# A softmax by blocks of token rows, a weight product in halves, and a new order of a planned stage

## The chip, the core and the metric

The kernel runs on one core of one Trainium2 chip. The metric is the device time of one execution in microseconds (us), the median over several runs. One further execution is recorded by the hardware profiler; its own time stands beside them below.

## The reference

```python
def _attn_ref(q, k, v, phi):            # 4 batches, 8 heads, 576 tokens, 64 columns, 32 memory slots
    a = softmax of phi over the tokens
    k_m, v_m = a^T k, a^T v              # pooled keys and values, 32 x 64 per head
    attn = softmax(scale * q k_m^T)      # over the 32 slots, for every token
    return attn v_m
x = attention, heads side by side       # 2304 tokens x 512
x = ((x w_a) * (x w_b)) w_out            # glu, inner width 1536
h = x w_in
return max(0.01 h, h) w_out2             # leaky, inner width 2048
```

All inputs are float32, and the kernel's planned stage and what follows split most operands into a high and a low part, so that three products (high by high, high by low, low by high) stand for one.

## The kernel before

The attention's last product and the glu's first are joined: with `vblk`, the pooled values, the kernel forms W = v_m w for each batch and each block f of 128 glu columns (`plan_w`, the product `wp`, L1183), and then one product of W with the attention weights AT gives (x w_a) and (x w_b) at once (`plan_ab`, the product `ab`, L1246, 24 of them per batch and block: two halves x of the width, two halves n of the tokens, two halves g of the heads, three passes). `copy` (ScalarE, L1263) and `mult` (VectorE, L1268) form the glu from it, and `x1p` (L1312) multiplies with w_out. W and AT are each made in two parts: ScalarE copies the high part (L1208, L1123), VectorE subtracts it for the low part (L1212, L1127).

The attention of one batch is `plan_att`. For batch 0 it pools keys and values (`km`, L771, first over k, then over v), scales them on ScalarE or VectorE (`kc`, L844, L846), turns them (`kvT`, L858) and writes `kk` and `vblk` (L882). Queries are turned in pieces (`qT`, L1014; `qL`, L970, for the last rows), the scores are `sc` (L1050, L1056), one group for each pair i of heads over all nine rows j of 64 tokens. VectorE takes the maximum (L993) and subtracts it (L1002), ScalarE forms the exponential (L1079) for two pairs at a time, VectorE sums (L1088), inverts and divides (L1100). Nine transposes `aT` (L1110), three to a bank, then bring the weights into AT. Each of these nine waits for the division of both halves of the heads.

The weights come as float32 in two halves of a word, and are joined after the load: ScalarE makes the high word (L438), GpSimd or ScalarE the low one (L446, L442), VectorE joins them (L456).

None of these instructions stands where the code names it. Each is a `Step` with an engine, a cost, what it waits for, and what it holds (a bank of `att`, `ab` or `wp`). `Plan.order` plays the steps through with these costs, and each engine gets its instructions in the order of the starts that come out. `LATE`, `FETCHED` and `LATEST` say how long after its issue a load is taken to land. `SEEDS` is a list of shuffles of the due times, applied one after the other. Where TensorE has nothing ready before 27 us, `run` puts in a product of ones (`warm`, L1680, 512 or 256 wide). Behind the planned stage, from L1690 on, the second layer is written out by hand.

```python
    LATE, FETCHED, LATEST = (4.0, 2.3), 1.2, 5.2
    WARM = 27.0
            s_at = add(PE, 0.325, att_t, s_soft, take=hold, uses=[s_users], kind="t")
```

## Time and profile before

| what | us |
|---|---|
| median of 3 runs | 738.47 |
| lowest, highest | 737.46, 738.53 |
| profiled execution, its own time | 738.45 |
| its span | 736.4 |
| TensorE busy (`warm` among it) | 729.4 |
| VectorE, ScalarE, GpSimd busy | 579.1, 413.7, 20.1 |

The span is the time between the first and the last instruction of the profile; the profiled execution's own time holds 2.05 us more, around it. A row of a timeline gives start, length, engine, line, operation, the tile written and the tiles read, and how many instructions are merged. A product of float32 operands shows twice in it, so that `x16` on `wp` is eight products. Neighbouring products overlap, and the distance from one start to the next is what one takes of the engine. A product with ones is a busy TensorE in all views.

### The profile page before, as it was taken

How to read it: one execution, taken by the hardware profiler on the slowest of the kernel's cores; microseconds unless marked ns; L12 is line 12 of the kernel's file. 1: busy time of each engine (PE TensorE's matmuls, PEld its weight loads, DVE VectorE, ACT ScalarE, POOL GpSimd, SP SyncE). 2: the span in 40 equal slices, each digit the busy share in tenths (PEclk: the TensorE clock that was granted, in tenths of full speed). 3: DMA queues.
4: the chain of work that ended last, by engine and by line, in shares of the span. 5: the costliest groups of instructions: out<-in, count | busy, mean ns of one | idle time of the engine just before them, and what ended most of it. 6: DMA issues, size and time to landing. Idle time of an engine off the chain costs nothing.

```text
span 736.4 us, 14535 instructions
## 1 busy us (share of the span) xinstructions
PE 729.4 (99%) x5391; PEld 654.2 (89%) x5391; DVE 579.1 (79%) x1196; ACT 413.7 (56%) x915; POOL 20.1 (3%) x38
## 2 busy tenths in 40 slices
PE   8999999999999999999999999999999999999997
PEld 5787887988889798888899999999999999999987
DVE  5987786967809999998746767998866997877797
ACT  3886684866729787856414455644444743454442
POOL 1210000001300000000000000000000000000000
PEclk9999999999999999999999999999999999999999
DMA  9995267474605989876527877778987777997493
GB/s 312 359 395 184 77 219 246 158 241 131 218 3 199 319 311 320 296 239 250 206 93 253 263 252 250 254 256 256 295 286 258 261 245 249 288 289 246 152 304 88
DMA packets 87495, 175.27 MB, mean 238 GB/s; under 512 B 7553, under 2 KB 36737, under 8 KB 87425
## 3 DMA queue, kind: packets, MB, share of 16 engines
q1 hardware_dynamic: 86736, 173.77, 70.6%
q8 instruction: 42, 0.69, 0.4%
q10 hardware_dynamic: 688, 0.59, 0.3%
q14 instruction: 29, 0.23, 0.1%
HBM read 140.25 MB, written 34.08 MB: 237 GB/s over the span
## 4 chain that ended last, share of the span: by engine, by line
PE 93%; DVE 3%; DMA 2%; ACT 1%; issue 0%; SPq 0%; DVEq 0%
PE h L1750 24%; PE x1p L1312 19%; PE ab L1246 19%; PE o L1850 15%; PE o L1854 8%; PE wp L1183 3%; DMA stage<-in_moe_w_b_dram 1%; PE sc L1050 1%; PE qT L1014 1%; PE km L758 1%; PE km L771 1%; PE aT L1110 1%; PE warm L1680 1%; DMA phi_t<-in_phi_dram 1%; DVE w2o L1434 0%; PE h L1825 0%
## 5 line engine op out<-in xcount | busy, mean ns | idle before, releaser
L1850 PE MATMUL o<-w2o,S 128*128 128x512 f32 (+1 forms) x504 | 177.1, 386 | 0.0
L1246 PEld LDWEIGHTS ab<-AT,W 128*128 128x128 f32 x1152 | 154.8, 188 | 7.0 <-ACT W L1208 2.5
L1246 PE MATMUL ab<-AT,W 128*128 128x288 f32 x1152 | 160.0, 297 | 0.2
L1312 PE MATMUL x1p<-G,wo 128*128 128x512 f32 (+1 forms) x720 | 156.5, 372 | 0.0
L1802 ACT ACTIVATE S<-g 128x384 fp32r<-128x384 f32 x168 | 87.6, 523 | 99.2 <-PE o L1850 85.9
L1312 PEld LDWEIGHTS x1p<-G,wo 128*128 128x128 f32 x720 | 123.5, 189 | 22.2 <-issue 0.8
L1750 PE MATMUL h<-T,ring 128*128 128x384 f32 x720 | 141.8, 335 | 0.0
L1854 PE MATMUL o<-w2o,S 128*128 128x256 f32 x492 | 137.6, 280 | 0.0
L1750 PEld LDWEIGHTS h<-T,ring 128*128 128x128 f32 x720 | 120.9, 188 | 4.1
L1803 DVE TENSOR_TENSOR S<-g,S 128x384 fp32r<-128x384 f32 x168 | 91.5, 553 | 40.4 <-ACT S L1802 40.2
L1850 PEld LDWEIGHTS o<-w2o,S 128*128 128x128 f32 x504 | 93.7, 188 | 14.5
L1854 PEld LDWEIGHTS o<-w2o,S 128*128 128x128 f32 x492 | 92.8, 189 | 0.0
L1872 DVE TENSOR_TENSOR C<-C,o 128x768 f32<-128x768 f32 x75 | 71.0, 949 | 13.9 <-ACT C L1876 7.9
L1750 PE MATMUL h<-B,ring 128*128 128x384 f32 x288 | 57.2, 336 | 0.0
L1793 DVE TENSOR_TENSOR g<-g 128x384 f32<-128x384 f32 x96 | 52.3, 552 | 2.9 <-ACT g L1760 2.4
L1750 PEld LDWEIGHTS h<-B,ring 128*128 128x128 f32 x288 | 48.8, 188 | 1.6
L438 ACT ACTIVATE stage<-stage 128x512 f32<-128x512 f32 x68 | 46.0, 686 | 5.6 <-DMA stage<-in_moe_w_in_dram 2.5
L1268 DVE TENSOR_TENSOR g<-a_sb,ab 128x288 f32<-128x288 f32 x96 | 42.1, 446 | 5.8 <-PE ab L1246 4.8
L1263 ACT COPY a_sb<-ab 128x288 f32<-128x288 f32 x96 | 38.3, 402 | 12.9 <-PE ab L1246 12.5
L1283 ACT ACTIVATE G<-g 128x576 fp32r<-128x576 f32 x48 | 33.2, 691 | 12.6 <-DVE g L1268 12.5
L1212 DVE TENSOR_TENSOR W<-wp,W 128x256 fp32r<-128x256 f32 (+1 forms) x75 | 35.1, 491 | 5.5 <-ACT W L1208 4.7
L1208 ACT ACTIVATE W<-wp 128x256 fp32r<-128x256 f32 (+1 forms) x75 | 30.3, 449 | 15.9 <-PE wp L1183 8.4
(143 smaller groups left out, 737.5 us busy)
## 6 DMA issues: line engine op xcount, KB each, us to landing
w2o<-a_scr SPq DMA_DIRECT2D x168, 256.0 KB, 3.8
ring<-a_scr SPq DMA_DIRECT2D x72, 512.0 KB, 4.4
stage<-in_moe_w_out_dram SPq DMA_DIRECT2D x28, 512.0 KB, 5.2
a_scr<-w2o SPq DMA_DIRECT2D x24, 512.0 KB, 3.7
a_scr<-a_out SPq DMA_DIRECT2D x24, 512.0 KB, 4.1
stage<-in_moe_w_in_dram SPq DMA_DIRECT2D x16, 512.0 KB, 5.2
stage<-in_moe_w_a_dram SPq DMA_DIRECT2D x12, 512.0 KB, 8.4
stage<-in_moe_w_b_dram SPq DMA_DIRECT2D x12, 512.0 KB, 7.5
```

The costliest lines, as they stand in the source:

```text
L438: act.activation(out=x, in_=x, func=ACTF.Prelu, scale=2.0 ** -112, alpha=2.0 ** 32)
L1246: pe.matmul(out=c[x, n][:, :HS], lhsT=W[b, f][:, hw, g, 128 * x:128 * x + 128], rhs=AT[b][:, g, ha, n * HS:(n + 1) * HS], start=(g == 0 an ...
L1263: act.copy(c["sb"][:, n], c[0, n][:, :HS])
L1268: dve.tensor_tensor(out=c["g"][:, n], in0=c["sb"][:, n], in1=c[1, n][:, :HS], op=ALU.mult)
L1312: pe.matmul(out=c["ps"], lhsT=wo_t[f][:, hw, 128 * m:128 * m + 128], rhs=G[f][:, hg, first:first + n], start=(f == fs[0] and (hw, hg) == P ...
L1750: pe.matmul(out=out, lhsT=ring[i % 2, part][:, o, kp, hw], rhs=x[:, hx], start=fresh and kp == 0 and (hw, hx) == PASSES[0], stop=kp == 1 a ...
L1793: dve.tensor_tensor(out=t, in0=x, in1=y, op=op)
L1802: act.activation(out=t[:, 0], in_=src, func=ACTF.Copy)
L1803: dve.tensor_tensor(out=t[:, 1], in0=src, in1=t[:, 0].bitcast(F32), op=ALU.subtract)
L1850: pe.matmul(out=dst[:, u, :y - x], lhsT=hi, rhs=wide[:, x:y], start=fresh and x == 0, stop=False, skip_group_check=True,)
L1854: pe.matmul(out=dst[:, u, :256], lhsT=lo, rhs=t[:, 0], start=False, stop=q == 3, skip_group_check=True,)
L1872: o_adds.append(lambda x=x: dve.tensor_tensor(out=total[name], in0=total[name], in1=x, op=ALU.add))
```

## The change

For batch 0 alone, `block(k)` does the softmax by rows of tokens and not by pairs of heads: rows 0 to 4 for all eight heads, then rows 5 to 8. Each block has two score groups (four pairs of heads, two pairs in a bank), its own sum, inverse and division. `qL` turns row 4 in place of row 8. The transposes `aT` go in groups of three, two and four rows, the first two waiting for the first block alone.

For the first block of the glu (b, f) = (0, 0), W is made in two halves, one for w_a and one for w_b, each with a tile of its own (`plan_w_first`), and its 24 products are no longer planned by three passes for each g, but by four steps: high by high for one g, the same for the other, low W by high AT for both, high W by low AT for both, and each waits for its own part.

`FETCHED` goes from 1.2 to 0.4 and `LATEST` from 5.2 to 4.8, and the list of shuffles is another, of 95 in place of 53. So the order changes throughout the planned stage. The code of the other batches is moved under an `else`.

```diff
-    LATE, FETCHED, LATEST = (4.0, 2.3), 1.2, 5.2
-    SEEDS = (683652, 560159, 530175, 125177, 433488, 159828, 165231, 686446, 405802, 158260, 349165, 253408, 67255,
...
-             250324)
+    LATE, FETCHED, LATEST = (4.0, 2.3), 0.4, 4.8
+    SEEDS = (522689, 898407, 926596, 464601, 390815, 382426, 130910, 244497, 699877, 414418, 82018, 903452, 136320,
...
+             532242, 848879, 434245, 992645)
...
-            def ql_t(i=i, n=n, hold=hold):
+            def ql_t(i=i, n=n, hold=hold, last=NR - 1 if b else 4):
...
-                        out=ps[:, 128 * x:128 * x + 128], in_=c["q"][:, i + x, (NR - 2) * D:NR * D], identity=ident
+                        out=ps[:, 128 * x:128 * x + 128], in_=c["q"][:, i + x, (last - 1) * D:(last + 1) * D],
+                        identity=ident,
...
-        for i in range(NQ):
-            hold = Hold(banks, 1)
-            qt_before, qt_users = qt0 if b == 0 else qt2 if i > 1 else plan.slot("qT", 2)
...
+        def block(k):
+            r0, nr = (0, 5) if k == 0 else (5, 4)
+            qt_before, qt_users = qt0
+            size = 2 * nr * M
+            s_ex = []
+            for h in range(2):
+                hold = Hold(banks, 1)
+
+                def q_t(h=h, hold=hold):
+                    ps = c["qTp", k, h] = bank(hold, "qT")
+                    for x in range(4):
+                        first = 128 * (2 * k + x % 2) + 64 * k
+                        pe.transpose(
+                            out=ps[:, 128 * x:128 * x + 128], in_=c["q"][:, 2 * h + x // 2, first:first + 128],
+                            identity=ident,
+                        )
+
...
+                    copy(
+                        c["qT"][:, 2 * h:2 * h + 2, 2 * k:2 * k + 2].rearrange("p i j x -> p i (j x)"),
+                        c["qTp", k, h].rearrange("p (i x) -> p i x", i=2),
+                    )
...
+                s = add(PE, 0.43, q_t, [ld_q[h]] + qt_before, take=hold, uses=[q_users], kind="t", n=8)
+                s_q = copied(q_copy, 512, [s] + qt_before, give=[hold], uses=[qt_users])
+                hold = Hold("att" if h else banks, 1)
...
+                def score(h=h, hold=hold):
+                    ps = bank(hold, "sc")[:, :size].rearrange("p (i x) -> p i x", i=2)
+                    for x in range(4):
+                        i, jj = 2 * h + x // 2, x % 2
+                        for g in range(NG):
+                            rows = slice(64 * g, 64 * g + 64)
+                            pe.matmul(
+                                out=ps[rows, x // 2, 64 * jj:64 * jj + 64], lhsT=c["qT"][:, i, 2 * k + jj, rows],
+                                rhs=kk[g][:, i].rearrange("p n m -> p (n m)"), start=True, stop=True,
+                            )
...
+                s_sc = add(
+                    PE, 0.22 if k else 0.33, score, s_kk + [s_q] + ([] if k else [s_ql[2 * h]]) + s_before, take=hold,
+                    uses=kk_users + [qt_users] + ([] if k else [ql_users]), n=16 if k else 24, kind="s"
+                )
...
+                    dve.tensor_reduce(out=c["m", k, h], in_=c["o", k, h], axis=AX.X, op=ALU.max)
+
+                s_max = add(DVE, t_dve(size), row_max, [s_sc] + m_before, uses=[m_users])
...
+                    return c["s"][:, r0:r0 + nr, 2 * h:2 * h + 2]
+
...
+                def less_row(h=h, part=part):
+                    bc = c["m", k, h].unsqueeze(3).to_broadcast([128, nr, 2, M])
+                    dve.tensor_tensor(out=part(), in0=c["o", k, h], in1=bc, op=ALU.subtract)
+
+                s_les = add(DVE, t_dve(size), less_row, [s_max] + s_before, give=[hold], uses=[s_users, m_users])
+                s_ex.append(add(
+                    ACT, t_act(size),
+                    lambda part=part: act.activation(out=part(), in_=part(), func=ACTF.Exp, scale=scale),
+                    [s_les], uses=[s_users],
+                ))
...
+                dve.tensor_reduce(out=c["m2", k], in_=c["s"][:, r0:r0 + nr], axis=AX.X, op=ALU.add)
+
+            s_rs = add(DVE, t_dve(2 * size), row_sum, s_ex + m_before, uses=[s_users, m_users])
+            s_eps = add(
...
+            def divide():
+                bc = c["m2", k].unsqueeze(3).to_broadcast([128, nr, NQ, M])
+                dve.tensor_tensor(
+                    out=c["s"][:, r0:r0 + nr], in0=c["s"][:, r0:r0 + nr], in1=bc, op=ALU.mult
+                )
+
+            return add(DVE, t_dve(2 * size), divide, [s_rec], port=True, uses=[s_users, m_users])
...
+        s_soft = []
+        if b == 0:
+            s_soft = [block(0), block(1)]
+            s_soft.insert(0, s_soft[0])
+        else:
+            for i in range(NQ):
...
-        for i in range(2):
-            part = slice(2 * i, 2 * i + 2)
-            s_ex = add(
-                ACT, t_act(576),
-                lambda part=part: act.activation(
-                    out=c["s"][:, :, part], in_=c["s"][:, :, part], func=ACTF.Exp, scale=scale
-                ),
-                s_att[part], uses=[s_users],
-            )
...
-        for i in range(3):
+        for i, (r0, nr) in enumerate(((0, 3), (3, 3), (6, 3)) if b else ((0, 3), (3, 2), (5, 4))):
...
-                for jj in range(3):
+                for jj in range(nr):
...
-            s_at = add(PE, 0.325, att_t, s_soft, take=hold, uses=[s_users], kind="t")
-            s_hi = add(ACT, t_act(384), high, [s_at], give=[hold])
-            ends += [s_hi, add(DVE, t_dve(384), low, [s_hi], give=[hold], early=8.0 if b else 0.0)]
+            s_at = add(PE, 0.108 * nr, att_t, s_soft if b else s_soft[i:i + 1], take=hold, uses=[s_users], kind="t")
+            s_hi = add(ACT, t_act(128 * nr), high, [s_at], give=[hold])
+            ends += [s_hi, add(DVE, t_dve(128 * nr), low, [s_hi], give=[hold], early=8.0 if b else 0.0)]
+        if b == 0:
+            att_ends.extend(ends)
...
-        for fs in ((0,), (1,)) if apart else ((0, 1),):
+        for fs, x in (((0,), 0), ((0,), 1), ((1,), None)) if apart else (((0, 1), None),):
             c = {}
-            where = "att" if apart and fs == (0,) else spot
+            where = "att" if apart and x != 1 else spot
             wide = where == "wp"
             holds = [Hold(where, 2 * len(fs)) for g in range(1 if wide else NG)]
...
+            made = [y for i in fs for n in range(2) if n == x or x is None for y in conv_end["wab", f + i, n]]
             s.append(main(
-                0.853 if len(fs) > 1 else 0.48, product, (ready if fs[-1] else ready[:NG]) + made + done_att + s, take=holds,
+                0.853 if len(fs) > 1 else 0.48 if x is None else 0.26, product, ready + made + done_att + s, take=holds,
...
-                def place(i=i):
+                def place(i=i, x=x):
+                    if x is not None and (b, f + i, x) not in W:
+                        W[b, f + i, x] = keep.tile([128, 2, NG, 128], F32R, tag=f"G{2 + x}", name="W")
+                    if x is not None:
+                        return W[b, f + i, x]
...
+    def plan_w_first(x):
+        s, high, low, holds, wide = w_before[0, 0, x]
+        before, users = plan.slot(f"G{2 + x}")
+        hi, lo = [], []
+        for k, hold in enumerate(holds):
+            n = 256 if wide else 128
+            hi.append(plan.add(ACT, 0.1 + t_act(n), lambda k=k: high(k), [s] + before, give=[hold], uses=[users]))
+            lo.append(plan.add(DVE, t_dve(n), lambda k=k: low(k), [hi[-1]], give=[hold], uses=[users]))
+        w_first[x] = hi, lo, users
 
     def plan_w_parts(b, f):
+        if (b, f) == (0, 0):
+            plan_w_first(0)
+            plan_w_first(1)
+            return
...
-            ends = [hi, lo] if k == 0 or (b, f) == (0, 0) else ends + [hi, lo]
-            for g in (k,) if (b, f) == (0, 0) else range(NG):
+            ends = [hi, lo] if k == 0 else ends + [hi, lo]
+            for g in range(NG):
                 w_end[b, f, g] = ends
...
-                    steps.append(main(
-                        0.3975, product, w_end[b, f, g] + att_end[b, g, n] + steps,
-                        take=None if g else out, uses=[w_used[b, f]],
-                    ))
+                    if (b, f) != (0, 0):
+                        steps.append(main(
+                            0.3975, product, w_end[b, f, g] + att_end[b, g, n] + steps,
+                            take=None if g else out, uses=[w_used[b, f]],
+                        ))
+                if (b, f) == (0, 0):
+
+                    def passes(todo, x=x, n=n, out=out):
+                        for g, hw, ha in todo:
+                            if todo[0] == (0, 0, 0):
+                                c[x, n] = bank(out, "ab")
+                            pe.matmul(
+                                out=c[x, n][:, :HS], lhsT=W[b, f, x][:, hw, g], rhs=AT[b][:, g, ha, n * HS:(n + 1) * HS],
+                                start=(g, hw, ha) == (0, 0, 0), stop=(g, hw, ha) == (1, 0, 1),
+                            )
+
+                    hi, lo, users = w_first[x]
+                    for todo, need in (
+                        ([(0, 0, 0)], hi[:1] + att_ends[2 * n:2 * n + 4:2]), ([(1, 0, 0)], hi),
+                        ([(0, 1, 0), (1, 1, 0)], lo), ([(0, 0, 1), (1, 0, 1)], att_ends[2 * n + 1:2 * n + 5:2]),
+                    ):
+                        steps.append(main(
+                            0.1325 * len(todo), lambda todo=todo, passes=passes: passes(todo), need + steps,
+                            take=None if steps else out, uses=[users], n=2 * len(todo),
+                        ))
```

On TensorE, around the first glu product, the order before is this, from the last score group on (`km` here pools v, `wp` is the product for f = 0 and then for f = 1):

```order
L1680 MATMUL warm<-const-float32-1.0 128x512
L1680 MATMUL warm<-const-float32-1.0 128x256
L771 MATMUL km<-kv_t,e 64x128 x36
L1680 MATMUL warm<-const-float32-1.0 128x256
L858 MATMUL kvT<-ident,kc 128x2x32 x2
L1680 MATMUL warm<-const-float32-1.0 128x256
L1183 MATMUL wp<-wab,vblk 32x256 x8
L1110 MATMUL aT<-ident,s 128x128 x9
L1680 MATMUL warm<-const-float32-1.0 128x256
L1183 MATMUL wp<-wab,vblk 32x256 x8
L1246 MATMUL ab<-AT,W 128x288 x36
L1183 MATMUL wp<-wab,vblk 32x512 x8
```

And after the change, the second `wp` of 16 instructions being the two halves for f = 0:

```order
L1831 MATMUL warm<-const-float32-1.0 128x512
L774 MATMUL km<-kv_t,e 64x128 x36
L1219 MATMUL aT<-ident,s 128x128 x3
L861 MATMUL kvT<-ident,kc 128x2x32 x2
L1219 MATMUL aT<-ident,s 128x128 x2
L1294 MATMUL wp<-wab,vblk 32x128 x16
L1219 MATMUL aT<-ident,s 128x128 x4
L1395 MATMUL ab<-AT,W 128x288 x12
L1294 MATMUL wp<-wab,vblk 32x256 x8
L1395 MATMUL ab<-AT,W 128x288 x10
L1376 MATMUL ab<-AT,W 128x288 x9
```

The first five transposes moved ahead of `wp`, into the places of two fillers, the last four stand right before the first `ab`, and the `wp` of f = 1 moved behind twelve of the products.

On VectorE, at the same place, before, from the last difference of a score on (`m` is the maximum and then the sum's inverse, `wab` a joined weight block):

```order
L1088 TENSOR_REDUCE m_323<-s 128x18
L1100 TENSOR_TENSOR s<-s,m_290 128x9x64
L1092 TENSOR_SCALAR m_323<-m_323 128x18
L1095 RECIPROCAL m_323<-m_323 128x18
L1100 TENSOR_TENSOR s<-s,m_323 128x9x64
L456 SCALAR_TENSOR_TENSOR wab<-stage 128x4x128
L1212 TENSOR_TENSOR W<-wp,W 128x256
L456 SCALAR_TENSOR_TENSOR wab<-stage 128x4x128
L1127 TENSOR_TENSOR AT<-aT,AT 128x3x2x64 x2
L1212 TENSOR_TENSOR W<-wp,W 128x256
L1127 TENSOR_TENSOR AT<-aT,AT 128x3x2x64
```

And after:

```order
L1106 TENSOR_TENSOR s<-s,m_288 128x640
L1094 TENSOR_REDUCE m_338<-s 128x16
L1098 TENSOR_SCALAR m_338<-m_338 128x16
L1101 RECIPROCAL m_338<-m_338 128x16
L459 SCALAR_TENSOR_TENSOR wab<-stage 128x4x128
L1106 TENSOR_TENSOR s<-s,m_338 128x512
L1236 TENSOR_TENSOR AT<-aT,AT 128x3x2x64
L1236 TENSOR_TENSOR AT<-aT,AT 128x2x2x64
L1327 TENSOR_TENSOR W<-wp,W 128x128 x2
L1327 TENSOR_TENSOR W<-wp,W 128x256
L459 SCALAR_TENSOR_TENSOR wab<-stage 128x4x128 x2
L1236 TENSOR_TENSOR AT<-aT,AT 128x4x2x64
```

The division is 640 and then 512 columns wide. A join of a weight block now stands between the second inverse and the second division, and the first differences of AT have moved ahead of those of W.

On ScalarE, from the last exponential on, before:

```order
L1079 ACTIVATE s<-s 128x9x64 x2
L844 ACTIVATE kc<-km,r 128x2x64 x2
L438 ACTIVATE stage<-stage 128x512
L882 COPY vblk<-kvT 128x128
L438 ACTIVATE stage<-stage 128x512
L1208 ACTIVATE W<-wp 128x256 x2
L1123 ACTIVATE AT<-aT 128x3x2x64 x2
L442 ACTIVATE stage<-stage 128x512
L1123 ACTIVATE AT<-aT 128x3x2x64
```

And after:

```order
L1085 ACTIVATE s<-s 128x4x64 x2
L847 ACTIVATE kc<-km,r 128x2x64 x2
L441 ACTIVATE stage<-stage 128x512
L1232 ACTIVATE AT<-aT 128x3x2x64
L885 COPY vblk<-kvT 128x128
L441 ACTIVATE stage<-stage 128x512
L1232 ACTIVATE AT<-aT 128x2x2x64
L1323 ACTIVATE W<-wp 128x128 x2
L1323 ACTIVATE W<-wp 128x256
L441 ACTIVATE stage<-stage 128x512
L1232 ACTIVATE AT<-aT 128x4x2x64
```

The high part of AT's first three rows moved ahead of the copy of `vblk`, and that of the next two ahead of W.

## Rows read from the trace of the kernel before

**Rows 1.** Head and part 1 of the page: busy time, share, instructions

```profile
span 736.4 us, 14535 instructions
...
PE 729.4 (99%) x5391; PEld 654.2 (89%) x5391; DVE 579.1 (79%) x1196; ACT 413.7 (56%) x915; POOL 20.1 (3%) x38
```

**Rows 2.** Waits of TensorE: who waited for whom; total, times, longest us

```profile
PE mxT L637 <- DVE mx L613: 1.0, 1, 1.0
...
PE kvT L858 <- ACT kc L844: 0.5, 1, 0.5
...
PE aT L1110 <- DVE s L1100: 0.2, 1, 0.2
```

**Rows 3.** Busy us by engine in two stretches, granted clock, DMA share, GB/s

```profile
27.09:382.05 354.96, 354.39 (x3030) 307.69 (x3023) 277.06 (x624) 238.34 (x556) 14.58 (x19) 1.00 0.64 223
...
4.00:6.00 2.00, 1.09 (x3) 0.19 (x1) 1.24 (x4) 0.00 (x0) 0.00 (x0) 1.00 0.98 322
```

**Rows 4.** Timeline of TensorE, 14 to 34 us

```profile
18.74 1.56 PE L1680 MATMUL warm<-const-float32-1.0 128*128 128x512 f32 x4
20.23 2.20 PE L771 MATMUL km<-kv_t,e 64*64 64x128 f32 x72
22.36 0.70 PE L1680 MATMUL warm<-const-float32-1.0 128*128 128x256 f32 x2
23.18 0.66 PE L858 MATMUL kvT<-ident,kc 128*128 128x64 f32 x4
23.67 0.65 PE L1680 MATMUL warm<-const-float32-1.0 128*128 128x256 f32 x2
24.25 0.66 PE L1183 MATMUL wp<-wab,vblk 64*32 64x256 f32 x16
24.85 1.20 PE L1110 MATMUL aT<-ident,s 128*128 128x128 f32 x9
25.89 0.60 PE L1680 MATMUL warm<-const-float32-1.0 128*128 128x256 f32 x2
26.50 0.67 PE L1183 MATMUL wp<-wab,vblk 64*32 64x256 f32 x16
27.09 5.47 PE L1246 MATMUL ab<-AT,W 128*128 128x288 f32 x36
32.50 1.09 PE L1183 MATMUL wp<-wab,vblk 64*32 64x512 f32 x16
```

**Rows 5.** Timeline of VectorE, 20 to 30 us

```profile
23.38 0.76 DVE L1100 TENSOR_TENSOR s<-s,m 128x576 f32<-128x576 f32 x1
24.06 0.68 DVE L456 SCALAR_TENSOR_TENSOR wab<-stage 128x512 int32<-128x512 int32 x1
25.42 0.42 DVE L1212 TENSOR_TENSOR W<-wp,W 128x256 fp32r<-128x256 f32 x1 [0.68 <-ACT W L1208]
...
26.36 1.01 DVE L1127 TENSOR_TENSOR AT<-aT,AT 128x384 fp32r<-128x384 f32 x2
```

**Rows 6.** Timeline of ScalarE, 22 to 29 us

```profile
22.50 0.62 ACT L844 ACTIVATE kc<-km,r 128x128 f32<-128x128 f32 x2 [1.31 <-PE km L771]
23.01 0.67 ACT L438 ACTIVATE stage<-stage 128x512 f32<-128x512 f32 x1
23.87 0.27 ACT L882 COPY vblk<-kvT 128x128 f32<-128x128 f32 x1 [0.19 <-PE kvT L858]
...
25.01 0.66 ACT L1208 ACTIVATE W<-wp 128x256 fp32r<-128x256 f32 x2 [0.26 <-PE wp L1183]
25.55 0.88 ACT L1123 ACTIVATE AT<-aT 128x384 fp32r<-128x384 f32 x2
```

**Rows 7.** Loads of v: issue ns and first, last start; KB, us to landing

```profile
L570 SPq DMA_DIRECT2D kv_t<-in_v_dram x2: 1391/1817/2243, 6.6 to 8.1; - x2
...
kv_t<-in_v_dram SPq DMA_DIRECT2D x1, 384.0 KB, 10.5
```

**Rows 8.** Waits of all engines, 27 to 360 us; same columns

```profile
ACT stage L438 <- DMA stage<-in_moe_w_in_dram: 2.5, 2, 1.7
```

203 lines of the change are left out of this document (121 added, 82 removed), and 9 rows, old and new, of the table SEEDS.

## The prediction

> **What bounds the kernel now.** I read the page's head first, then TensorE's waits, then the start by its timelines. TensorE is busy for 729.4 of 736.4 us [rows 1]; its longest named waits are 1.0 and 0.5 us, before 13 us, and the one of 0.2 is the longest behind 27 us [rows 2]. From the first glu product (27.09) to the end of the planned stage (382.05) it idles 0.57 of 354.96 us [rows 3]. The change leaves the number of products after the start as it is and touches nothing of the hand-written stage behind 382 us. So it can only gain where TensorE is busy with nothing useful: the fillers (`warm`) before 27.09. They count as busy, but each stands where the plan had nothing to run. From the last score on there are the 512 and 256 wide ones at 18.74, then 256 wide ones at 22.36, 23.67 and 25.89 [rows 4]: 1.49 + 0.82 + 0.58 + 0.61 = 3.5 us, each taken to the start of the next row (the second one with 0.1 of the wait for kc in it). That is the whole prize, and only the part whose cause is removed can be won.
>
> What ends last there? The first `ab` needs three things: W (from `wp`, which needs the pooled values vblk), the attention weights AT (from the transposes `aT`, which need the softmax), and the second `wp`, which stands before it in TensorE's order. The second half's softmax is divided at 23.38 to 24.14 [rows 5], vblk is written at 23.87 to 24.14 [rows 6]; both come to the same moment. Nine transposes then take 24.85 to 25.89 and the copies and differences of AT and W fill VectorE and ScalarE to 27.4 [rows 4 to 6]. So two chains of equal length bound the start, and shortening one alone brings little.
>
> **The change, part by part.** All sums are against the profiled execution, 738.45 us (span 736.4 and 2.05 around it); the median of the three runs is 738.47, the same within 0.02.
>
> *Pooled values.* The loads of v are issued in the same place. Their second half is issued at 8.1 and takes 10.5 us, so it lands at 18.6 [rows 7]; the product stands at 20.23 because TensorE comes to it then. In the new order four score groups and the same 512 and 256 wide fillers stand ahead of it. Bounds: 18.6 (landing) and 20.9 (20.23 and one high-word step of 0.67 [rows 6] that comes ahead of a ScalarE copy for which a score group waits). I take 20.3, next to the row. From its start to vblk it was 24.14 - 20.23 = 3.9 us [rows 4, 6]; now ScalarE copies the first AT piece (three token rows) ahead of vblk, 0.88 / 2 = 0.44 [rows 6], of which the 0.19 that ScalarE idled before vblk hides a part. So vblk is ready at 20.3 + 3.9 + 0.2 = 24.4, 0.3 later than before. This part alone is a loss.
>
> *Softmax by token rows.* Five rows go first for all heads. Their division is done before the pooled product ends, so `aT` of the first five rows fills TensorE's wait for kc and vblk, where the 256 wide fillers stood; that hides 5 of the 9 transposes. The last four rows come later than the old second half: in VectorE's new order the join of a weight block (0.68) stands in front of their division, and it needs a ScalarE step (0.67) queued behind kc. kc ends at 23.12 before [rows 6], 0.1 later now: 23.2; the step overlaps its neighbours and ends at 23.8; the join ends at 24.5; the division, 512 columns instead of 576, 0.69 (from 0.76), at 25.15; four transposes with their wait 0.5 (nine took 1.04): 25.7.
>
> *First W in halves, products by passes.* The halves of `wp` take 0.6 (24.25 to 24.85) and lie between vblk and these transposes: 24.45 to 25.05, beside the division. W high is copied by 25.9 in three ScalarE pieces (0.66 for two of 256 before), the first two by 25.6. With passes, the first `ab` needs W high and AT high alone, not the differences. It starts at 25.75, 1.34 before 27.09.
>
> *What is late next.* The second `wp` (f = 1) now stands behind 12 products, because its last weight join follows the differences on VectorE: two AT pieces (1.01 for two of 384; now 384 and 256, 0.85), three W pieces (0.42 for 256 columns, so about 0.2 + 0.2 + 0.35 overlapped), one join (0.68): from 25.1 to about 27.3. The 12 products take 12 x 0.135 = 1.6 from 25.75, to 27.4: they just cover that wait. If they stop short of it, each 0.1 us of VectorE's delay is paid. `wp` and the change into the next kind of product take 0.6 (26.50 to 27.09): 28.0 for the 13th product. Before, the 36 products from 27.09 took 5.41 to the next row, 0.150 each, so the 13th stood at 28.9. **Gain of the start: 0.9 us**, with 0.3 to 2.0 as its ends (pooled product at 20.9 or at 18.6, where from 24.0 on the differences and not v hold the products).
>
> On VectorE's and ScalarE's pieces the rows give a 256-column difference 0.42 and a 512-column division some 0.69, so a piece costs about 0.15 before its first column, and one piece more on each engine is 0.15. The Trainium skill speaks against such cuts (VectorE: DVE Perf Modes, section "The TRN2 errata"): every instruction pays a fixed latency, so tiles of 512 elements and more are advised. By it nothing overlaps between pieces and the start would lose some 0.3 of the gain; but the two AT pieces took 1.01 together [rows 5], less than twice one alone, so I keep the pitch.
>
> *New order behind the start.* The new constant and the new list of shuffles move instructions all through the plan. The order has 96 changes between kinds of product behind the first `ab`, before 88. Nine transposes and the change into them took 1.04 [rows 4], under 0.12 each, so a change costs 0 to 0.1; eight more: 0 to 0.8, taken as 0.1, since the old 88 fit into a stretch with 0.57 idle. The instructions of VectorE and ScalarE stay the same in kind but for the pieces above, and three low-word steps of ScalarE moved to GpSimd. What can be won there is bounded by the 0.57 of idle time. Loads are planned with 0.4 to 0.8 us less time to land (the two constants), but the landing is not set by the table. I take 0 for both.
>
> Sum: 738.45 - 0.9 + 0.1 = **737.6 us**.
>
> **Rivals.** *Pooled product early (736.2).* If the score groups finish by 18.5, v is the gate and every step above but VectorE's moves 1.5 us up; the gain is then bounded by the row blocks and comes to about 2.2. For it: the first score no longer stands behind the third transposed q tile. Against it: a 512 wide filler is written in front of the product.
>
> *The start stays (738.4).* If the division of the last four rows slips to 26.4 behind the join, first `ab` and second `wp` come where they were, and the change does not do what it says. For it: the chain above has two engines in series ahead of that division. Against it: 1.2 us of slip that no row shows.
>
> *Slower: an engine's queue held by a load (740.9).* Weight steps of ScalarE stand ahead of the copies that free product banks. If a step is placed before its load has landed, TensorE runs out of four banks. Before, ScalarE waited so for 2.5 us in all on one kind of load, 1.7 at the longest [rows 8], and TensorE's banks covered it. Two such waits with no cover are 3.4: 738.45 - 0.9 + 3.4 = 740.9. It decides from the point where a load lands more than about 2 us after its step's turn; with 0.8 less in the table one or two of the later loads could come to that, but TensorE shows no idle for any today.
>
> *Slower: the clock falls (about 742).* Three fillers fewer make TensorE less busy before 27 us. The granted clock stood at 1.00 (2.4 GHz) even from 4 to 6 us, where TensorE was busy 1.09 of 2.00 [rows 3], and my longest new idle time is 0.3. At the lower level, 1.2 GHz, the 4 to 5 us of true products between 20.3 and 28 would take twice as long. The Trainium skill has this rule (TensorE: Matmul & The Clock Gate, Part 1): an idle array falls back to half its clock. By it the time would be that of this rival; the trace so far shows no fall.
>
> **How the numbers follow.** Forecast 737.6: 0.58 (own range 736.9 to 738.3). Pooled product early: 0.20. Start stays: 0.08. Queue held: 0.12. Clock: 0.02. The range for 8 in 10 reaches to the middle of the early case and into the held case, which need not be full: 736.2 to 739.1. About 0.2%, 1.48 us, is what a measurement of this kernel tells from no change: faster means under 737.0. Most of the early case and a tenth of the forecast's lie there: 0.26. Slower than 739.9: the two last cases, 0.12 after a light held case is taken off. The same: 0.62.
>
> **What would show it.** Right: first `ab` near 25.8 and 13th near 28.0, the pooled product of v at 20.0 to 20.6, vblk later than 24.14, the division of four rows ending near 25.2 right before the last four transposes; behind 30 us every TensorE time about 0.9 earlier than before, and idle under 1 us to the end of the plan. Wrong: the pooled product at 19 (then the early case), a wait of TensorE on `wp` of f = 1 that the 12 products do not cover, any wait over 0.5 us behind 30 us, or a clock under 1.00. The forecast is wrong by its main step if TensorE's lead at 30 us is not the lead at the end.

## The result and the profile after

The changed kernel takes 742.72 us (median of 6, 740.74 to 744.40) where the kernel before takes 738.37 (median of 6, 737.46 to 738.73): 1.0058 times as long, 95% interval 1.0036 to 1.0080. The forecast was 737.6 with a range up to 739.1, so it is missed by 5 us and on the wrong side. The profiled execution took 744.08, with a span of 741.2.

The executions of the changed kernel lie apart by more than those of the kernel before, and their mean granted clock goes with it: 740.74, 740.79 and 741.57 have 1.000, while 743.87, 744.08 and 744.40 have 0.994 to 0.998. The traced execution is one of the latter. Of the 5.63 us between the two traced executions 4.8 lie in the span; the time around it is 2.9 us here and was 2.05 before, and no trace shows why.

The head, part 1 and one queue of part 3 of the page of after (beside [rows 1]):

```profile
span 741.2 us, 14550 instructions
...
PE 731.0 (99%) x5401; PEld 655.1 (88%) x5401; DVE 580.2 (78%) x1197; ACT 414.0 (56%) x917; POOL 21.6 (3%) x41
...
q8 instruction: 42, 0.69, 0.4%
```

TensorE has 10 records more and is busy 1.6 us longer, but the span is 4.8 us longer. So 3.2 us are idle time that the kernel before did not have. The list of TensorE's waits, after (who waited for whom; total, times, longest us; beside [rows 2]), says where:

```profile
PE km L761 <- issue: 2.3, 1, 2.3
PE kvT L861 <- DVE kc L849: 0.9, 1, 0.9
...
PE aT L1219 <- DVE s L1106: 0.4, 1, 0.4
```

The first row is new and the longest of all. "Issue" means that no engine and no transfer of the profile released it. The timeline of TensorE around it, after (start us, length, line, operation; the idle time ahead and its releaser in brackets):

```profile
154.07 2.22 PE L761 MATMUL km<-kv_t,phi_t 64*32 64x128 f32 x141
158.56 0.54 PE L761 MATMUL km<-kv_t,phi_t 64*32 64x128 f32 x3 [2.27 <-issue]
159.02 0.59 PE L897 MATMUL km<-ones,es 128*128 128x2 f32 x2
159.47 2.85 PE L1463 MATMUL x1p<-G,wo 128*128 128x512 f32 x6
```

and the stretches of the stop and behind it (us, busy us and records of PE, PEld, DVE, ACT, POOL; granted clock, DMA share, GB/s):

```profile
154.00:158.60 4.60, 2.33 (x144) 2.01 (x144) 2.22 (x6) 0.69 (x1) 0.00 (x0) 1.00 0.96 334
158.60:162.10 3.50, 3.50 (x11) 2.56 (x11) 0.33 (x2) 1.74 (x5) 0.00 (x0) 0.51 0.98 305
```

The pooled product of the fourth batch (`km`, L761) runs 141 of its 144 small products, stands still for 2.27 us, and goes on. Behind that the granted clock is 0.51, which is the level of 1.2 GHz, and six `x1p` products take 2.68 us from the first start to the start of the next row, 0.45 each, where they take 0.2345 at 2.4 GHz.

The whole account, by the distance from one start to the next, from the start of the first `ab` to the start of the last `x1p`, where the forecast put the end of the planned stage: 354.96 us before (27.09 to 382.05), 360.23 after (26.56 to 386.79). Of the 5.27 more, `km` has 2.89, `x1p` 1.86, `wp` 0.60 (its second product, f = 1, now stands behind the first `ab`), `ab` 0.41, and the other kinds together 0.5 less. TensorE's part of the hand-written stage behind it takes 350.5 in both.

The start, after (timeline of TensorE, beside [rows 4]):

```profile
19.31 0.69 PE L1046 MATMUL sc<-kk,qT 128*64 128x64 f32 x16
19.93 1.13 PE L1831 MATMUL warm<-const-float32-1.0 128*128 128x512 f32 x2
20.99 2.19 PE L774 MATMUL km<-kv_t,e 64*64 64x128 f32 x72
...
26.09 0.63 PE L1219 MATMUL aT<-ident,s 128*128 128x128 f32 x4 [0.41 <-DVE s L1106]
26.56 1.89 PE L1395 MATMUL ab<-AT,W 128*128 128x288 f32 x12
28.49 0.67 PE L1294 MATMUL wp<-wab,vblk 64*32 64x256 f32 x16
29.09 1.18 PE L1395 MATMUL ab<-AT,W 128*128 128x288 f32 x5
```

The first `ab` comes 0.53 us earlier than before, but the 13th stands at 29.09, where it stood at 29.00 before. The 0.9 us that the forecast put here are not there.

So there are two questions: what stops TensorE at 156 us, and what holds the start.

### The profile page after: what moved, and what is told of

It reads as the page before. It is cut to its first block, busy times and chain, and to the rows that moved or that the text cites. A ratio compares the mean times of both kernels' runs of the same rounds, so it can differ in the third digit from the quotient of the medians.

```text
span 741.2 us, 14550 instructions
## 1 busy us (share of the span) xinstructions
PE 731.0 (99%) x5401; PEld 655.1 (88%) x5401; DVE 580.2 (78%) x1197; ACT 414.0 (56%) x917; POOL 21.6 (3%) x41
## 4 chain that ended last, share of the span: by engine, by line
PE 93%; DMA 3%; DVE 1%; ACT 1%; issue 1%; SPq 0%; DVEq 0%; ACTq 0%
PE h L1901 24%; PE x1p L1463 20%; PE ab L1376 18%; PE o L2001 15%; PE o L2005 8%; PE wp L1294 3%; DMA phi_t<-in_phi_dram 1%; DMA stage<-in_moe_w_out_dram 1%; DMA kv_t<-in_k_dram 1%; PE sc L1160 1%; PE km L761 1%; PE qT L1124 1%; PE km L774 1%; PE aT L1219 1%; PE h L1976 0%
## 5 line engine op out<-in xcount | busy, mean ns | idle before, releaser
L1376 PE MATMUL ab<-AT,W 128*128 128x288 f32 x1128 | 155.9, 297 | 0.2
L1376 PEld LDWEIGHTS ab<-AT,W 128*128 128x128 f32 x1128 | 151.4, 188 | 3.6 <-issue 0.8
L2023 DVE TENSOR_TENSOR C<-C,o 128x768 f32<-128x768 f32 x75 | 71.0, 949 | 13.9 <-ACT C L2027 7.9
L1438 DVE TENSOR_TENSOR G<-g,G 128x576 fp32r<-128x576 f32 x48 | 37.2, 775 | 3.6 <-ACT G L1434 3.4
L1323 ACT ACTIVATE W<-wp 128x256 fp32r<-128x256 f32 (+2 forms) x77 | 30.7, 442 | 13.8 <-PE wp L1294 6.9
```

Source lines behind the costliest of these rows:

```text
L1376: pe.matmul(out=c[x, n][:, :HS], lhsT=W[b, f][:, hw, g, 128 * x:128 * x + 128], rhs=AT[b][:, g, ha, n * HS:(n + 1) * HS], start=(g == 0 an ...
L2023: o_adds.append(lambda x=x: dve.tensor_tensor(out=total[name], in0=total[name], in1=x, op=ALU.add))
```

## What stops TensorE: a count of instructions

Theory A: TensorE had used up the instructions that had been brought to it. The queue q8 brings them: 42 packets with 0.69 MB in the whole run, 16.4 KB each, for 10,802 products and weight loads of TensorE, about 256 per packet. The Trainium skill (Trainium Architecture — The Big Picture, section "The software stack") gives 64 bytes for an instruction, which agrees: 256 of them are 16,384 bytes. The same place names the move of the streams to the engines when the program is loaded, and no other. Here packets come all through the run as well, and the trace decides. The pooled product is the fastest consumer in the kernel: 288 instructions in 2.2 us. Theory B: the stop is a wait on data, or on a transfer, that the profile does not name.

The planner knows of this. `run` cuts TensorE's program into blocks of 256 (`BLOCK`), lets a block be there 4.8 us after the one before it was entered (6.9 us up to 50 us of the plan), and counts each step's instructions by its `n`. The change enters its new score steps with `n=24` and `n=16`. The steps hold 12 and 8 products, which show as 24 and 16 in the trace, each with a weight load: 48 and 32 instructions. The kernel before had `n=40` for 10 products, which is right. So from the first batch on, the planner of the change is 80 instructions behind the program, and it put the fourth batch's pooled product where by its count the ends of the blocks did no harm. That is read from the code: no run changes `n` alone.

**The changed kernel again.**

> The changed kernel once more, to stand beside the others on the same chip. Its trace showed TensorE stop for 2.27 us inside the pooled product of the fourth batch (after 141 of its 144 small products, 156.3 to 158.6 us) with no releaser, and the granted clock at 0.5 for 3.4 us right behind. Theory A (instructions: TensorE used up the instructions it had, and the next stretch had not been brought): the stop has the same place in every execution, after product 141, 2 to 3 us; the clock falls behind it in some executions, which then take some 743.5 to 744.5, the others 740.5 to 741.6. Theory B (data or transfers: a wait that the trace does not name, or the weight loads that run at that time): the stop moves by microseconds or differs in length between executions. Both: median 740.7 to 744.

Measured: 742.99 (median of 8, 740.79 to 745.17), 1.0049 times before (739.14 on this chip), interval 1.0032 to 1.0066. The stop is there again, at the same product and within 0.02 us of the same length (timeline of TensorE):

```profile
154.72 2.21 PE L761 MATMUL km<-kv_t,phi_t 64*32 64x128 f32 x141
159.19 0.41 PE L761 MATMUL km<-kv_t,phi_t 64*32 64x128 f32 x3 [2.25 <-issue]
```

The place is the same in both traces, as A says, and the clock fell behind it again. In the two shortest executions the clock is 1.000 and 0.999 (740.79 and 741.09); what they look like inside no trace shows.

**96 instructions more, by doubled scores.** In `score`, for the third batch:

```
-                            pe.matmul(
+                            for _ in range(2 if b == 2 and i < 3 else 1):
+                                pe.matmul(
```

> The changed kernel with 24 of the third batch's score products written twice (same operands, same result), 96 TensorE instructions more between the pooled products of the third and the fourth batch, nothing else moved. Theory A: the end of the stretch of instructions comes 96 instructions earlier in the pooled product of the fourth batch, after some 93 of its 144 products, and its request lies some 35 products of the glu's second half ahead, so it is there in time: no stop over 0.3 us, clock 1.00 throughout, all executions within 1 us, median 739.9 to 740.9 (the repeats themselves cost 48 x 7 ns = 0.34). Theory B: the stop of 2.3 us stays, with the fall of the clock in some executions: median 742.7 + 0.3 = 743.0 as before, in two groups 3 us apart.

Measured: 742.04 (median of 10, 739.87 to 744.46), 1.0032, interval 1.0017 to 1.0046. In its trace the pooled product runs through (1.98 us from first to last start) and the clock stays at 1.00, span 738.5; but that execution was one of the quick ones (740.29), and the median lies between A's 740.9 and B's 743.0, a little nearer to B's. A second trace of the same kernel tells why:

> One more execution with its trace of the changed kernel with 96 instructions more. Its ten executions took 739.9 to 744.5, and the one that left a trace was of the quick ones (740.3) and showed neither the stop nor a fall of the clock. Theory A (the stop and the fall behind it are all of the difference between executions): it shows neither again and takes 740 to 741. Theory E (the plan reckons its loads to land sooner, and in executions in which they land later TensorE waits for what needs them): where it takes 742 or more, TensorE shows waits of 0.5 us and more on copies, joins or loads behind 30 us that the quick execution does not show, with the loads' landing 1 to 2 us later than there, and no stop in the pooled product.

Measured: 742.08 (5 executions, 741.58 to 745.55). The traced one took 742.08. It has no stop in the pooled product, but one in the scores that the edit itself had made denser (timeline of TensorE):

```profile
113.67 1.18 PE L1161 MATMUL sc<-kk,qT 128*64 128x64 f32 x32
116.02 0.31 PE L1167 MATMUL sc<-kk,qL 128*64 128x32 f32 x4 [1.17 <-issue]
```

No wait of TensorE on a load or a copy grew by 0.5 us or more, except `mxT` at 52 us (0.9 for 0.4), ahead of which two VectorE instructions took longer (1.16 for 0.68 and 0.99 for 0.55) with no load between. So theory E, late loads, is not what the trace shows. The edit had cured one stop and made another.

**The same number in the kernel before.** The same edit with 10 and with 32 score products there:

> The kernel before with 10 of the third batch's score products written twice: 40 TensorE instructions more ahead of the fourth batch's pooled product, nothing else moved. Theory A: the end of a stretch, which by the count of the changed kernel lies some 15 products behind that pooled product here, comes inside it, and TensorE stops for 2 to 2.6 us near 152 us in a kernel that had no such stop: 738.4 + 0.14 + 2.5 = 741.0, and some 3 more in executions in which the clock falls. Theory B: the loads and the data are the same, so no stop: 738.4 + 0.1 = 738.5.

> The kernel before with all 32 of these score products written twice: 128 TensorE instructions more, three times as many as in the run with 40. Theory A: the end of the stretch now lies early in the fourth batch's pooled product and the next one far behind it: no stop, 738.4 + 0.45 = 738.9, less than with 40 instructions more, in spite of more work. Theory B: 738.4 + 0.45 = 738.9 too, but more than with 40 instructions.

Measured: 740.37 (1.0018, interval 1.0009 to 1.0028) with 40 more and 740.36 (1.0015, 1.0007 to 1.0024) with 128 more. With 40 the pooled product stops after 139 of 144 products, as A says, but for 0.4 us of idle time (0.7 from start to start) and not for 2.5. With 128 it doesn't stop. That the second is no faster in spite of that fits its longer scores (9.28 us for 7.37 before, 1.9 more, where 0.45 was expected), so the medians tell nothing apart. The place does.

**Spread edits.** The next two add the instructions as products of 2 columns at the start of long groups:

```
+    def spare(ps):
+        for _ in range(2 if len(pooled) == 2 and small[0] > 0 else 0):
+            small[0] -= 1
+            pe.matmul(out=ps[:NG, :NG], lhsT=ones[:32, :NG], rhs=ones[:32, :NG], start=True, stop=True)
```

> The changed kernel with 96 TensorE instructions more ahead of the fourth batch's pooled product, this time not inside the score products (doubled scores ran out of instructions themselves: a stop of 1.4 us at 116.0 in one trace) but as 24 products of 2 columns, two each at the start of twelve groups of long products; their results are overwritten. Theory A (TensorE stops where a dense piece of small products reaches the end of the instructions that are there, and the clock falls behind a long stop): no stop over 0.3 us in the pooled products or the scores, clock 1.00 in every execution, median 740.2 to 741.2 (the start's loss and the smaller waits of the order, 1.2 + 1.0, stay: 739.0 + 2.2 = 741.2 at most), beside 743 for the changed kernel. Theory E (late loads make the slow executions): median 742 and some of them at 743 to 744, as with the doubled scores.

> The kernel before with 40 TensorE instructions more ahead of the fourth batch's pooled product, as 10 products of 2 columns spread over five groups of long products. Theory A: the pooled product stops at the same count of instructions as in the changed kernel (number 3519 or 3520, after 139 to 141 of its 144 products), for 0.7 us where the loads rest and for up to 2.5 where they run: 739.0 + 0.1 + 0.7 to 2.5 = 739.8 to 741.6. Theory B (place set by the data or by the new order): no stop, 739.1.

Measured: 742.81 (1.0050, 1.0033 to 1.0068) and 741.43 (1.0028, 1.0017 to 1.0038). The changed kernel has no stop and a clock of 1.00 in its trace, but the 48 records of 2 columns take 42 ns each on average (26 from one to the next, 89 from the last of four into the long product), 2.0 us, and the account from the first `ab` to the last `x1p` is 3.2 us longer than that of the split products below. The expectation had not priced this, and its median was missed: 742.81 lies where theory E had it, so this run alone doesn't tell A from E. The kernel before stops again after 139 products, 0.6 us idle.

**Products split in two.** The last pair adds the instructions for 0.0065 us each, by writing 512 wide products of `x1p` as two of 256:

```
-                    pe.matmul(
-                        out=c["ps"],
...
+                    for part in parts(n, (f, hw, hg) in ((fs[0], *PASSES[0]), (fs[-1], *PASSES[-1]))):
+                        pe.matmul(
+                            out=c["ps"][:, part],
```

> The changed kernel with 96 TensorE instructions more between the third and the fourth batch's pooled products at nearly no price: 48 of the 512 wide products of the glu's second half are written as two of 256 columns (0.1205 us each in the trace, one of 512 takes 0.2345: 48 x 0.0065 = 0.3 us). Theory A (all that made the change slow is the stop, with the fall of the clock): no stop, clock 1.00, planned stage ends at 382.6 to 383.2 instead of 386.8, median 739.7 to 740.3, within 0.2% of the kernel before (739.1 to 739.2 on this chip). Theory E (late loads): 742, with executions 3 us apart.

> The kernel before with 20 such products split: 40 TensorE instructions more for 20 x 0.0065 = 0.13 us (the products of 2 columns took 42 ns a record and a change of kind each, 0.9 us and more, and the doubled scores 0.3). Theory A: the pooled product of the fourth batch stops at instruction 3519 or 3520 for 0.6 to 0.9 us, as in the two runs with 40: 739.1 + 0.13 + 0.6 to 0.9 = 739.8 to 740.2. Theory B: no stop, 739.2.

Measured: 740.13 (median of 11, 738.88 to 740.90; 1.0009, interval 1.0000 to 1.0019) and 740.38 (1.0015, 1.0005 to 1.0024). The first is where A put it, and not near E's 742; the second is 0.2 over A's range and far from B's 739.2. Two of the eleven executions of the first, 740.86 and 740.90, have a clock of 0.998 or less, and the traced one is the quickest, 738.88. The changed kernel with 96 instructions more (timeline of TensorE):

```profile
153.97 2.25 PE L770 MATMUL km<-kv_t,phi_t 64*32 64x128 f32 x144
156.15 0.38 PE L906 MATMUL km<-ones,es 128*128 128x2 f32 x2
```

The planned stage ends at 382.65 and not at 386.79. The kernel before with 40 more:

```profile
151.03 2.20 PE L767 MATMUL km<-kv_t,phi_t 64*32 64x128 f32 x139
153.91 0.41 PE L767 MATMUL km<-kv_t,phi_t 64*32 64x128 f32 x5 [0.69 <-issue]
```

**The count itself.** A stretch from 0 to just before a stop's end, in five traces (columns as above; the number behind PE's time is the products so far). The changed kernel, and again:

```profile
0.00:158.50 158.50, 152.12 (x1740) 125.33 (x1741) 123.43 (x273) 102.69 (x228) 13.29 (x29) 1.00 0.69 239
```

```profile
0.00:159.10 159.10, 152.41 (x1740) 126.49 (x1741) 122.54 (x273) 102.92 (x228) 14.06 (x29) 0.99 0.69 238
```

The kernel before with 40 more, by split and by 2 column products:

```profile
0.00:153.85 153.85, 150.64 (x1739) 125.10 (x1739) 120.62 (x269) 102.54 (x225) 10.39 (x25) 1.00 0.68 235
```

```profile
0.00:155.30 155.30, 152.76 (x1739) 124.95 (x1739) 122.45 (x269) 102.58 (x225) 10.63 (x25) 1.00 0.67 233
```

The changed kernel with doubled scores, second trace:

```profile
0.00:116.00 116.00, 109.57 (x1358) 89.32 (x1359) 88.73 (x192) 74.15 (x163) 13.74 (x29) 1.00 0.74 255
```

Programs with different orders stop after 1,740, 1,740, 1,739 and 1,739 products. The stop in the scores comes after 1,358. That is 382 fewer, which are 764 instructions with their weight loads; 4 waits of TensorE's own sequencer that the trace lists between make 768, three times 256. The trace without the filler (in the next section), with two fewer ahead of the scores, stops in them after 1,358 as well. With the sequencer's waits, the first four stops come after 3,520, 3,520, 3,521 and 3,521 instructions. By the same count the fourth batch's pooled product ends with instruction 3,490 in the kernel before, 30 short of the block's end, and with 3,525 after the change, 5 behind it. Data, loads and orders differ; the number is the same. Theory B falls, and A is shown: TensorE stops at the end of a block of 256 instructions when it runs through a block faster than the next one comes.

**How long.** Seven traces have such a stop: the five above, the kernel before with 40 more by doubled scores, and the changed kernel with doubled scores and without the filler. In all seven TensorE goes on 1.4 to 1.5 us after the q8 packet has landed (in the first the packet runs from 156.11 to 157.04, and TensorE goes on at 158.56). What differs is when the packet starts, counted from TensorE's entry into the block ahead: 1.9 us in both traces of the changed kernel, 3.4 and 3.2 in the two that stop in the scores, 0.1 to 0.4 in the three of the kernel before with 40 more. So the changed kernel stopped for 2.27 us, and the kernel before with 40 more for 0.4 to 0.7. In the first four, stores and loads were in full flow in the 2 us behind that entry (DMA share 0.99 to 1.07), in the last three not (0.14 to 0.15). That the transfers hold the packet up is not shown. Over the three pooled products of all seventeen traces the packet starts 0.1 to 1.3 us behind the entry where that share is up to 0.32 (21 cases), 0.9 to 1.8 at 0.38 to 0.83 (16), and 0.9 to 3.6 at 0.91 and more (14): with busy DMA engines it can come late or not, and an experiment with the transfers taken away wasn't tried.

## What holds the start: one filler

Theory C: the pooled product of v (L774) starts the chain of the start. In the changed kernel it comes at 20.99, behind a 512 wide filler of 1.06 us, with v landed at 19.5. `kc`, the high-word step, the join, the division, the last transposes and the first `ab` follow one another from it. Theory D: the loads hold the start, and nothing comes of taking the filler away.

```
         warmed.append(n)
+        if len(warmed) != 8:
             pe.matmul(out=warm_ps[:, :n], lhsT=unit[:, :128], rhs=unit[:, :n], start=True, stop=True)
```

> The changed kernel with the 96 TensorE instructions more (no stop in the fourth batch's pooled product in its trace) and, beside that, without the 512 wide filler that stands ahead of the pooled product of the first batch's v (1.06 us of TensorE in all three traces of this order: 19.93 to 20.99 in the first). Theory C (the start is held by this product: kc, the high-word step behind it on ScalarE, the join and the division of the last four rows on VectorE, the last four transposes and the first glu products follow one another from it): the product comes up to 1.0 us earlier, bounded by the landing of v (19.5 to 21.3 in the three traces), so the first glu product near 25.6 to 26.2 instead of 26.6 and the time 0.4 to 1.0 under that with 96 more: 741.0 to 741.6 at the median. Theory D (the start is held by the loads): TensorE waits for v where the filler stood, first glu product at 26.6, time unchanged at 742.0; the idle array may lose its clock, then 743.

> The kernel before without the 512 wide filler ahead of the pooled product of v (18.74 to 19.8 in its trace), nothing else moved. Theory C: the product at 19.2 to 19.5 instead of 20.23, vblk at 23.2 instead of 24.14, the softmax's second half (divided at 24.14) then sets the start: first glu product 0.3 to 0.7 earlier, 738.4 to 738.8 beside 739.1 of before on this chip. Theory D: v lands at 18.6 to 20.6 in the traces of this order, so it is waited for, and nothing is won: 739.1, or slower where the clock falls.

Measured: 740.47 (median of 12, 739.22 to 743.35; 1.0027, interval 1.0015 to 1.0038) beside 742.04 and 742.08 with the filler, and the first `ab` at 25.46 for 26.66, the 13th at 27.91 for 29.10 (timeline of TensorE without the filler):

```profile
19.97 2.20 PE L774 MATMUL km<-kv_t,e 64*64 64x128 f32 x72
...
25.46 1.89 PE L1396 MATMUL ab<-AT,W 128*128 128x288 f32 x12
27.29 0.70 PE L1295 MATMUL wp<-wab,vblk 64*32 64x256 f32 x16
27.91 1.66 PE L1396 MATMUL ab<-AT,W 128*128 128x288 f32 x10
```

C holds in the changed kernel, and the median is under the 741.0 that it gave as the lower end: its 1.6 is more than the 1.2 us that the trace shows, and both kernels have the stop in the scores in some executions. In the kernel before the same cut gives 738.82, 0.9997 times (0.9986 to 1.0007): nothing. There the first `ab` moves from 27.09 to 27.00 only, with `aT` now waiting 0.46 us for the division:

```profile
24.84 1.20 PE L1110 MATMUL aT<-ident,s 128*128 128x128 f32 x9 [0.46 <-DVE s L1100]
...
27.00 1.24 PE L1246 MATMUL ab<-AT,W 128*128 128x288 f32 x6
```

So before, the softmax was as late as the pooled product, as the prediction said, and the change did take the softmax off that place.

Split products and no filler together:

> The same without the 512 wide filler ahead of the pooled product of the first batch's v. With the doubled scores this took 1.2 us off the first glu product (25.46 for 26.66) and 1.0 off the lost time at 50 us, and the median went from 742.0 to 740.5. Theory C: 0.8 to 1.2 below the run before, 738.6 to 739.4, level with the kernel before. Theory D: as the run before.

Measured: 738.41 (median of 12, 737.58 to 741.07; 0.9994, interval 0.9981 to 1.0008), 0.2 under the lower end of theory C. Seven executions took 737.6 to 738.5, five 739.8 to 741.1 with a clock of 0.997 or 0.998. The traced one is of the five (stretches of TensorE, and the two waits in its timeline):

```profile
5.00:14.00 9.00, 6.72 (x95) 4.32 (x93) 4.93 (x13) 2.40 (x5) 0.00 (x0) 1.00 1.04 352
14.00:18.50 4.50, 4.50 (x44) 4.11 (x44) 1.70 (x5) 1.54 (x3) 1.31 (x2) 0.62 1.08 353
```

```profile
9.72 2.20 PE L783 MATMUL km<-kv_t,e 64*64 64x128 f32 x72 [1.06 <-DMA kv_t<-in_k_dram]
...
13.87 1.08 PE L870 MATMUL kvT<-ident,kc 128*128 128x64 f32 x8 [0.90 <-DVE kc L858]
```

The clock is at its lower level from 14.9 to 18.3, right behind the wait for `kc`. In the second trace of the changed kernel it is so from 13.9 to 17.3, behind the same wait:

```profile
13.90:17.30 3.40, 3.40 (x35) 3.01 (x34) 1.18 (x4) 1.54 (x3) 1.31 (x2) 0.50 1.08 357
```

Six other traces have this wait too, of 0.85 to 0.93 us, and keep a clock of 1.00 behind it, the first of the changed kernel among them (wait 0.9, clock 1.00 from 8 to 18). So the wait does not bring the fall each time. The new start has a wait of 0.9 for `kc` where the old one had 0.5 [rows 2]. The last kernel puts a filler into that wait:

```
                 def mem_t(g=g, n=n, hold=hold_t):
+                    if "kvT" not in done:
+                        done.add("kvT")
+                        warm(256)
```

> The changed kernel with 48 products split (96 instructions more), without the 512 wide filler ahead of the pooled product of v, and with a 256 wide one in TensorE's 0.9 us wait for kc at 12.5 us instead. Without the latter, 7 of 12 executions took 737.6 to 738.5 at a clock of 0.999 or 1.000 and 5 took 739.8 to 741.1 at 0.997 or 0.998; the one that left a trace was of those and had the clock at 0.5 from 14.9 to 18.3 us, behind waits of 1.1 us for k and 0.9 for kc. Theory H (that fall comes from the idle time ahead of 14 us): fewer or no executions over 739.5, median 737.8 to 738.3, 0.1 to 0.2% under the kernel before (739.1). Rival (the fall has another cause, or k lands too late for one filler to help): as without it, 738.4 with executions at 740 and above.

Measured: **737.86** (median of 10, 737.07 to 738.82), 0.9981 times the kernel before (739.24 here), interval 0.9971 to 0.9990. All ten executions have a clock of 1.000. That is what theory H expected. It rests on falls in 0 of 10 executions against 5 of 12, on two chips, so it is likely rather than proven. This version is 0.19% shorter than the kernel before, by an interval that excludes 1; of its 1.4 us, 0.9 are in the span (medians 736.1 and 737.0), and the rest is time around it that no trace explains. Its start (timeline of TensorE):

```profile
12.23 0.60 PE L1848 MATMUL warm<-const-float32-1.0 128*128 128x256 f32 x2
13.28 1.08 PE L873 MATMUL kvT<-ident,kc 128*128 128x64 f32 x8 [0.45 <-DVE kc L858]
...
19.84 2.20 PE L783 MATMUL km<-kv_t,e 64*64 64x128 f32 x72
...
25.38 1.88 PE L1407 MATMUL ab<-AT,W 128*128 128x288 f32 x12
27.19 0.71 PE L1306 MATMUL wp<-wab,vblk 64*32 64x256 f32 x16
27.84 1.65 PE L1407 MATMUL ab<-AT,W 128*128 128x288 f32 x10
```

## The planner with the right count

Could the plan have been right from the start? Both codes were planned anew with the block ends moved by 51 instructions to where the stops show them and a new list of shuffles, and the changed one with `n=48` and `n=32` and the old load constants besides. So the planner of the kernel before was off by these 51 as well, and its 30 instructions of room are no merit of its count:

```
-                    ... n=16 if k else 24, kind="s"
+                    ... n=32 if k else 48, kind="s"
...
+            if t >= self.START and not moved:
+                moved.append(made[0])
+                made[0] += self.MORE
```

> The changed kernel's code planned anew: the first batch's score steps entered with the 48 and 32 instructions that they have (24 and 16 in the change), the planner's ends of blocks moved by 51 instructions to where the stops showed them, before's reckoning of the loads (1.2 and 5.2), and a list of shuffles sought for that with the planner's own end as the measure (379.95, beside 380.45 of the next run). Theory F (the change is worth what the planner thinks, once it counts right): no stop, 0.5 under the next run, 737.5 to 738.8. Theory G (its start costs what the trace showed: the second W product behind the twelfth glu product, 0.6 more lost at 30 us than before): not faster than the next run, 738.6 to 740.

> The code of the kernel before, planned anew in the same way: ends of blocks moved by 51 instructions, a new list of shuffles (planner's end 380.45). It tells the code of the change from the luck of the order. Theory F: 0.5 above the run before, 738.0 to 739.3. Theory G: level with the kernel before or better, 738.3 to 739.3, and not above the replanned change.

Measured: 741.74 (1.0030, 1.0018 to 1.0042) and 739.64 (1.0002, 0.9992 to 1.0012). Neither stops on a block in its trace. Both lie above the ranges of both theories. Theory F falls: the planner's own end had the replanned change 0.5 us ahead, and it is 2.1 behind. In the trace of the replanned change the `ab` products take 158.5 us from start to start, 2.0 more than the 156.5 of the other, most of it in 16 more steps of over 0.2 us where one takes 0.13; its start also has fillers in front of the pooled product of v, 1.9 us of them (13th `ab` at 29.97). One list of shuffles each, so this does not tell the code of the change from the luck of its order. It tells that the planner's end is no measure at half a microsecond.

## Why the prediction was wrong, step by step

*The step that failed most* is "New order behind the start", a term put at 0 for the new table and the new shuffles, which bounded only what could be won ("bounded by the 0.57 of idle time"). A loss had no bound, and that the count of instructions sets where TensorE can run on was not among the forecast's waits at all. In the runs this term is about 4.2 us. The stop is 2.5 us of it from start to start, and the fall of the clock behind it about 1.6: the account of the changed kernel and that of the split one differ by 4.2 us between the starts of the first `ab` and the last `x1p` once the 0.3 of the splits is taken off, (386.79 - 26.56) - (382.65 - 26.29 - 0.31) = 4.18. What the trace of before could have shown is that its pooled products take 288 instructions in 2.2 us and that q8 brings a packet during each; and the diff shows an `n` that is half of what the step emits. Neither was read.

*Pooled values.* Taken at 20.3 between 18.6 and 20.9, it came at 20.99: just outside the bound. The same filler stands ahead of it, but the last score ends at 19.93 and not at 18.74, as two groups of query transposes now stand between the score groups, where one did, and `kvT` waits 0.9 for `kc`. From there on everything is late by 0.6 to 0.8: the division ends at 25.94 (25.15 forecast), the first `ab` at 26.56 (25.75).

*Softmax by rows, W in halves.* The mechanism was right: five transposes fill the wait, the division of the last four rows stands behind the join, the second `wp` comes behind 12 products, which cover its wait. Mis-sized are the 12 products (1.93 for 1.6) and the start of the chain. The forecast priced these products at 0.135 each, which no row gives, and the same products before at 0.150, so 0.2 of its 0.9 came from two prices for one thing. With the filler gone the 13th `ab` is at 27.84 and 27.91 in the two traces that keep the clock there (29.85 in the one where it falls), and the forecast had 28.0. So the gain of 0.9 was to be had, behind a filler that the forecast had named as what speaks against it, in "Pooled product early", and had not priced in the forecast itself.

*Rivals.* "The clock falls (about 742)" came nearest in time, at a chance of 0.02 and for another place and cause, so that is luck: the forecast looked for idle time of the start and saw at most 0.3. The Trainium skill's rule on the idle array (TensorE: Matmul & The Clock Gate, Part 1), cited there, agrees with these traces: 2.27 and 2.25 us of standing still were followed by the lower level. Stops of 0.45 to 1.26 us were not. "Queue held by a load" is not there: ScalarE's longest wait on one weight load behind 27 us is 1.8 as before 1.7 [rows 8], and TensorE does not wait for it. "The start stays" is what is left when the stop is gone: 740.13 beside 739.2, 0.6 of it without the price of the splits.

*What would show it* named the right sign: "any wait over 0.5 us behind 30 us, or a clock under 1.00".

## What to carry to other kernels

In this kernel a piece of small products uses up instructions faster than they are brought, so where the ends of the instruction blocks fall is part of a schedule: count what a step really emits, and after any edit ahead of a dense piece look for a wait on "issue" inside it. To test for it, shift the program by some instructions at little cost, for instance by splitting long products (0.0065 us each here), and see whether the stop moves by as many. A stop of 2 us can cost over one and a half times its length, since the clock may fall behind it.

## What the hardware showed unexpectedly

TensorE's instructions are brought during the run, 16.4 KB at a time (42 packets, 0.69 MB), and a stop came at the same count in programs with different orders (1,739 or 1,740 products, and 764 instructions and 4 waits earlier, 768 = 3 x 256). TensorE goes on 1.4 to 1.5 us after the packet has landed.

The clock fell behind 2.27 and 2.25 us without a product, and in two traces behind a wait of 0.9 us at 12 to 14 us. It did not fall behind stops of 0.45 to 1.26 us in five traces, behind the same wait of 0.9 in six others, nor at 4 to 6 us in the kernel before with TensorE busy for 1.09 of 2.00 [rows 3].

Products of 2 columns are not free: 26 ns from one to the next and 42 on average with the step into the long product, where the small products of the pooled values take 15.
